# One planner, new durations, new due times: a reordered attention and feed-forward kernel

## The chip, the cores and the metric

One core of a Trainium2 chip runs the whole program. The metric is the device time of one execution in microseconds. The kernel before was timed three times: 1012.86, 1009.65 and 1012.70 us, median 1012.7 us.

## The reference

There are two computations, one behind the other.

```python
# attention with random features; q, k, v are 8 x 8 x 576 x 64, omega is 128 x 64
def phi(x):
    proj = einsum('bhsd,md->bhsm', x, omega)
    h = proj - sum(x * x, -1) / 2
    return exp(h - max(h, -1)) / sqrt(128)
q_p, k_p = phi(q * scale), phi(k * scale)
kv = einsum('bhsm,bhsd->bhmd', k_p, v);  z = sum(k_p, axis=2)
x = einsum('bhsm,bhmd->bhsd', q_p, kv) / (einsum('bhsm,bhm->bhs', q_p, z) + 1e-6)
# feed-forward on x as 4608 tokens x 512; w_in 512 x 2048, w_out 2048 x 512 (float64 inputs)
h = x @ w_in
out = where(h > 0, h, exp(min(h, 0)) - 1) @ w_out
```

## The kernel before

**What is computed where.** The attention goes by 32 pairs of heads (`pair`): load, project k and q (`project`), sum over the keys (`kv`), normalise and form the output (`finish`). The first eight pairs do it in one way (plain fp32 matmuls, L491, L665, L781), the other 24 in another (operands split in a high and a low part, L541, then L609 and L829). The feed-forward takes 3072 tokens in eight blocks of 384: for each of 16 slices of the hidden size a step does 12 matmuls of 384 columns (`layer1`, L969 to L971: high by high, high by low, low by high), ReLU, exponential and two splits on ACT and DVE, and 9 matmuls of 512 columns (`layer2`, L1003 to L1005). The first three blocks are done in two halves of eight steps each, while the weights are still converted from float64 words (`from_f64`). The last 1536 tokens go by three groups of 512 in eight steps each (`wide1`, `wide2`, L1354, L1324, L1512): a form with seven instead of eight products, of 84 matmuls of 256 columns a step. What it needs is built before it from the weights in `prepare` (tiles `rw`, `w1t`) and `prepare2` (tiles `tw`), and `fetch` brings three 512 KB weight tiles (`wp`) for each step through three buffers.

**What sets the order.** Nothing in the code above is issued where it stands. Each operation is handed to a planner, `Plan.op(engine, ns, due, fn, reads, writes, ...)`, with a duration for each engine that may do it and a due time. `Plan.order` plays a schedule through with these durations: each engine takes, whenever it is free, the ready operation with the earliest due time, if its buffers are free. Its outcome is a fixed order of instructions on each engine, and the engine for those that name another one in `alt`. The chip then runs that order. The durations come from small formulas: `mm` for matmuls, `act`, `dve`, `pool`, and single numbers at the call. The due times come from a nominal time line (`MLP0`, `SEG`, `STEP`, ...), with offsets for each stage (`PD0`, `PDS`: the pairs from the ninth on; `PREP0`, `TWO0`; `UNIT0`, `UNIT1`; `FETCH`; `AT`, `BT`: products within a step). Only their differences matter, since a due time is compared with nothing but other due times. `ALT` holds a handicap in us for each kind of operation: another engine is taken only if it ends earlier by that much. With `port=True` DVE and POOL are planned never to run such operations at the same time. DMAs are planned as 1.1 us, bytes at 360 per ns, and another 1.1 us.

Of the kernel before, what the change touches and what calls it, by code (L numbers as in the profile page):

```python
# [9 lines left out]
F32 = mybir.dt.float32  # L10
# [8 lines left out]
P = 128  # L19
# [8 lines left out]
TB = 384  # L28
NTT = TB // P
NBLK = 8  # L30
TOK0 = NBLK * TB
SB = 512
# [27 lines left out]
PREP0, PREP = -101.339, 8.8  # L60
TWO0, TWO = -37.142, 7.995
SUM = 0.873
UNIT0, UNIT1 = 0.25, 3.77
FETCH = 14.688
BT = [-0.751, -0.373, 0.719, 0.06, 0.525, 0.7, 0.865, -0.155, -0.328, 1.177, -1.344, 0.575, -1.141, 0.489]
AT = (0.0, 0.337, 0.844, 0.312, 0.229, 0.181, 0.386)

LAG = 3.4


PAIR0 = 6.45
# [221 lines left out]

ALT = dict(kv=1.96, out=2.95, conv_clamp=13.06, conv_hi=14.02, conv_sub=16.5, g_hi=12.75, g_lo=11.74, y_hi=None, y_lo=0.82, norm=18.01, p2=0.03, unit=-5.32, unit_hi=0.48, prep=0.118, part=5.545, q_hi=1.554, q_lo=14.04, neg=7.821, turn=0.31, x_hi=0.28, sq=-0.48, two=-0.272, two_hi=0.343, sum=0.079, s_hi=0.129, s_lo=0.3, zero=-0.108)

# [5 lines left out]
def mm(n, m=1):  # L301

    return m * (n / 2.4 + 2.5)

# [9 lines left out]
def pool(n):  # L314
    return 40 + 2.33 * n


@with_exitstack
def performer_elu_kernel(
# [131 lines left out]
    def project(i, nm, due):  # L451
# [14 lines left out]
        if native(i, nm):  # L466
# [11 lines left out]
            for g in range(3):  # L478
# [16 lines left out]

                op("PE", 872 if g < 2 else 240, d, mms, [*((x, a, 2) for a in range(2)), of], (p,))
                op(
# [20 lines left out]
        for a in range(2):  # L518
            r, o = slice(a * D, a * D + D), slice(D - a * D, P - a * D)
            cs = slice(a * S, a * S + S)  # L520
            parts = ((x, 0),)
            op(
                "ACT", act(S), due - 5 + a, lambda e, r=r, cs=cs: copy(e, y()[r, cs], x()[r, 0]), parts, ((y, a, "h"),),
                alt=other("y_hi", "DVE", dve(S, True)), port=True,
            )
            op(
                "POOL", pool(S), due - 4 + a,
                lambda e, r=r, o=o, cs=cs: tt(e, y()[o, cs], x()[r, 0], y()[r, cs].bitcast(F32), ALU.subtract),
                (*parts, (y, a, "h")), ((y, a, "l"),), alt=other("y_lo", "DVE", dve(S)), port=True,
            )  # L530
        for c in range(5):
# [13 lines left out]

            op("PE", mm(256, n), d, mms, [(y, a, z) for a in range(2) for z in "hl"] + ["oh", "om"], (p,))
            op(
# [13 lines left out]
            if c in (1, 4):  # L561
# [6 lines left out]

                op("POOL", 2 * pool(4), d + 1.3, bias, [sq, *((nb, g, e) for e in range(5))], ((nb, g),))
                exps(g, js, lambda j: h()[:, j, :], d + 1.5, [(h, g, e) for e in range(5)])  # L570
# [27 lines left out]
    def kv_swapped(i, due):  # L598
# [34 lines left out]

        op("POOL", 3 * pool(2 * M) + 2 * pool(M), due + 0.5, sums, parts, (zs, (zu, 1)))
        op("ACT", act(M), due + 2.8, lambda e: copy(e, zu()[:, 0], zs()[D:P, 0]), (zs,), ((zu, 0),), alt=other("kv", "DVE", dve(M, True)), port=True)
# [12 lines left out]
    def kv(i, due):  # L648
# [21 lines left out]
        parts = parts_of(i, "k")  # L670
        op("PE", 220, due, last, [*parts, v], ((p, 0), (p, 1)))
        for a in range(2):
# [16 lines left out]
    def finish(i, due):  # L689
# [25 lines left out]
        for g in range(3):  # L715
# [67 lines left out]
        d = due - 2  # L783
        op("PE", 4 * mm(S) + 200, d, mms, [*((qh, g) for g in range(3)), ("kvf", i % 2)], [p for _, _, p in halves])
        for half, (qs, n, p) in enumerate(halves):
# [28 lines left out]
    def output(i, qt, due):  # L814
# [8 lines left out]
        def mms():  # L823
# [9 lines left out]
        op(  # L833
            "PE", 4 * mm(4 * N) + 200, due, mms, [*((qt, g) for g in range(3)), *((zk, "kv", e) for e in range(4))], banks
        )
# [120 lines left out]
    def layer1(F, due):  # L956
        blk, f = STEPS[F][:2]
        o = (SLOT[blk] if blk > 2 else blk) * TB
        w = w1c.pop(F)
        p = Buf(ps, [P, 512], F32, "ph", f"ph_{F}", 2)  # L960
        e = Buf(sb, [P, TB], F32, "e", f"e_{F}", 2)
        g = gt[F] = [Buf(sb, [P, 512], F32R, "g", f"g_{F}_{z}", 6) for z in range(2)]

        def ph():
            return p()[:, 0:TB]

        def mms(c):
            wh, wl = w()[:, 0, c * P:(c + 1) * P], w()[:, 1, c * P:(c + 1) * P]
            nc.tensor.matmul(ph(), wh, xh[:, c, o:o + TB], start=(c == 0), stop=False)  # L969
            nc.tensor.matmul(ph(), wh, xl[:, c, o:o + TB], start=False, stop=False)  # L970
            nc.tensor.matmul(ph(), wl, xh[:, c, o:o + TB], start=False, stop=(c == NC - 1))  # L971

        for c in range(NC):
            reads = [("x3h", SLOT[blk], c), ("x3l", SLOT[blk], c)] if blk > 2 else [(z, k) for k in ring(blk) if k[1] == c for z in ("xh", "xl")]
            op("PE", mm(TB, 3), due + 0.5 * c, lambda c=c: mms(c), [*reads, (w, "h"), (w, "l")], (p, ("f", blk, f)) if c == 0 else (p, ("fl", blk, f)) if c == 3 else (p,))
        due += 2

        op("ACT", act(TB, True), due, lambda: nc.scalar.activation(e(), ph(), AF.Relu, scale=-1.0), (p,), (e,))  # L978
        op("ACT", act(TB), due + 0.2, lambda: nc.scalar.activation(e(), e(), AF.Exp, scale=-1.0), (e,), (e,))  # L979
# [13 lines left out]

    def layer2(F, due):
        blk, f, f0, f1 = STEPS[F]
        g = gt.pop(F)
        for tt in range(NTT):
            if f == f0:
# [188 lines left out]
    def std_x(blk, due):  # L1187

        X = [Buf(sb, [P, NJ, M], F32, "h", f"xs_{blk}_{k}", 4) for k in range(2)]

        def x(k):
            return X[k]().rearrange("p j x -> p (j x)")[:, 0:2 * TB].rearrange("p (c x) -> p c x", c=2)

        t0, o = blk * TB, SLOT[blk] * TB
        for k in range(2):
            op(
                "SP", 500, due + 0.1 * k,
                lambda k=k: nc.sync.dma_start(x(k), xd[2 * k:2 * k + 2, :, t0:t0 + TB].rearrange("c p x -> p c x")),
                [("xd", b * NHP + hp) for b in range(B) if b * S < t0 + TB and t0 < b * S + S for hp in (2 * k, 2 * k + 1)]
                + [("f", blk - 1, 11)], (X[k],), P * TB * 8,  # L1200
            )
            first = SLOT[blk] not in list(SLOT.values())[:blk - 3]
            keys = [z for z in ring(SLOT[blk]) if z[1] in (2 * k, 2 * k + 1)] if first else []
            xk = [z[:, 2 * k:2 * k + 2, o:o + TB] for z in (xh, xl)]
            heads, tails = ([(nm, SLOT[blk], c) for c in (2 * k, 2 * k + 1)] for nm in ("x3h", "x3l"))
            op(
                "ACT", act(2 * TB), due + UNIT0 + 0.5 * k, lambda e, k=k, xk=xk: copy(e, xk[0], x(k)), (X[k],),
                [*(("xh", z) for z in keys), *heads], alt=other("unit_hi", "DVE", dve(2 * TB, True)), port=True,
            )
            op(  # L1210
                "POOL", pool(2 * TB), due + UNIT0 + 0.4 + 0.5 * k,
                lambda e, k=k, xk=xk: tt(e, xk[1], x(k), xk[0].bitcast(F32), ALU.subtract), (X[k], *heads),
                [*(("xl", z) for z in keys), *tails], alt=other("unit", "DVE", dve(2 * TB)), port=True,
            )
# [487 lines left out]
```

## Time and profile before

| | |
|---|---|
| median of three executions | 1012.7 us |
| span of the profiled execution, first to last instruction | 1006.4 us |
| what lies around the span, against the median | 6.3 us |
| PE busy | 981.2 us (97%), 7806 matmuls |
| DVE, ACT, POOL busy | 842.0, 765.8, 557.6 us |
| granted TensorE clock, mean | 1.000 |

PE is the matmul engine, PEld its weight loads, DVE, ACT and POOL the vector, scalar and GpSimd engines, SP the one that issues DMAs. A matmul's duration in the trace is longer than its distance to the next one, since matmuls are pipelined and their ends are modelled: a busy PE can hide short waits. The pace of a kind of matmul is the distance from start to start in an unbroken run.

### The profile page before, as it was taken

The numbers are of one execution on the slowest core, as the hardware profiler recorded it, in microseconds if no ns is written. First come the engines' busy times: TensorE is split into PE (matmuls) and PEld (weight loads), VectorE is DVE, ScalarE is ACT, GpSimd is POOL, SyncE is SP. The second block draws the span as 40 slices with busy tenths as digits, with TensorE's granted clock in tenths as the row PEclk, the third lists the DMA queues.
The fourth block names the chain that finished last, engine by engine and source line by source line (L and its number), as shares of the span: only waits on it lengthen the run. The fifth ranks groups of instructions, "written<-read, shape, count | busy, mean of one in ns | idle before, by whom it ended". The sixth has DMA issues, their size and how long they took to land.

```text
span 1006.4 us, 24315 instructions
## 1 busy us (share of the span) xinstructions
PE 981.2 (97%) x7806; PEld 883.9 (88%) x7806; DVE 842.0 (84%) x3077; ACT 765.8 (76%) x2064; POOL 557.6 (55%) x745
## 2 busy tenths in 40 slices
PE   7999999999999999999999999999999999999997
PEld 7788788878888888888888888888789999999997
DVE  7999977887778788878888888889999889779766
ACT  7989777777668888888787778776546788777774
POOL 2667666685547767677577766684442232223221
PEclk9999999999999999999999999999999999999999
DMA  7656787757776776676666766767878876766752
GB/s 230 174 191 198 232 276 262 249 185 236 232 246 202 236 229 204 210 240 207 223 211 220 237 196 211 231 218 236 295 272 309 294 264 205 233 219 193 220 200 66
DMA packets 93264, 226.27 MB, mean 225 GB/s; under 512 B 23056, under 2 KB 35024, under 8 KB 93136
## 3 DMA queue, kind: packets, MB, share of 16 engines
q1 hardware_dynamic: 93136, 224.70, 68.8%
q8 instruction: 63, 1.03, 0.4%
q14 instruction: 65, 0.53, 0.2%
HBM read 187.43 MB, written 37.22 MB: 223 GB/s over the span
## 4 chain that ended last, share of the span: by engine, by line
PE 68%; DVE 15%; DMA 6%; ACT 5%; issue 3%; POOL 3%; SPq 1%; DVEq 0%; POOLq 0%; ACTq 0%
PE acs L1512 9%; PE ph L969 6%; PE ph L971 6%; PE acc L1003 6%; PE ph L970 6%; PE A L1354 6%; PE acc L1005 6%; PE acc L1004 6%; PE B L1354 4%; PE pkv L609 2%; PE pn L829 2%; PE ppq L541 2%; PE ppk L541 2%; DVE junk L727 1%; DVE u_w L914 1%
## 5 line engine op out<-in xcount | busy, mean ns | idle before, releaser
L969 PE MATMUL ph<-xh,w1c 128*128 128x384 f32 x512 | 176.9, 345 | 6.3 <-DVE g L990 4.4
L970 PE MATMUL ph<-xl,w1c 128*128 128x384 f32 x512 | 172.3, 336 | 1.0 <-DVE xl L794 1.0
L971 PE MATMUL ph<-xh,w1c 128*128 128x384 f32 x512 | 172.3, 336 | 0.0
L1003 PE MATMUL acc<-w2h,g 128*128 128x512 f32 x384 | 154.6, 402 | 0.1
L1005 PE MATMUL acc<-w2h,g 128*128 128x512 f32 x384 | 151.6, 395 | 0.0
L1004 PE MATMUL acc<-w2l,g 128*128 128x512 f32 x384 | 151.3, 394 | 0.0
L969 PEld LDWEIGHTS ph<-xh,w1c 128*128 128x128 f32 x512 | 96.2, 188 | 18.7 <-DVE g L990 8.5
L970 PEld LDWEIGHTS ph<-xl,w1c 128*128 128x128 f32 x512 | 96.3, 188 | 3.8 <-DVE xl L794 1.4
L978 ACT ACTIVATE e<-ph 128x384 f32<-128x384 f32 x128 | 62.5, 488 | 47.5 <-PE ph L971 47.0
L381 POOL TENSOR_TENSOR hq<-hq,den 128x512 f32<-128x512 f32 (+1 forms) x96 | 80.9, 852 | 28.7 <-DVE den L736 23.2
L971 PEld LDWEIGHTS ph<-xh,w1c 128*128 128x128 f32 x512 | 96.2, 188 | 0.0
L982 DVE SCALAR_TENSOR_TENSOR ph<-e,ph 128x384 f32<-128x384 f32 x128 | 71.3, 557 | 27.4 <-ACT e L979 26.1
L381 POOL TENSOR_TENSOR gq<-yh,gq 128x256 fp32r<-128x256 f32 x49 | 42.8, 873 | 87.0 <-ACT gq L376 76.8
L1005 PEld LDWEIGHTS acc<-w2h,g 128*128 128x128 f32 x384 | 72.0, 188 | 17.1
L1003 PEld LDWEIGHTS acc<-w2h,g 128*128 128x128 f32 x384 | 72.1, 188 | 16.2 <-issue 6.3
L727 DVE CUSTOM_DVE_ANT_0 junk<-hq,pz 128x128 f32<-128x128 f32 (+1 forms) x320 | 74.6, 279 | 12.7 <-PE pz L705 10.6
L381 POOL TENSOR_TENSOR tk<-xk,tk 64x576 fp32r<-64x576 f32 x45 | 64.1, 1424 | 32.2 <-ACT tk L376 14.9
L461 ACT ACTIVATE hk<-hk,nbk 128x128 f32<-128x128 f32 x216 | 68.4, 391 | 15.7 <-POOL nbk L567 15.3
L1004 PEld LDWEIGHTS acc<-w2l,g 128*128 128x128 f32 x384 | 72.2, 188 | 8.7
L461 ACT ACTIVATE hq<-hq,nbq 128x128 f32<-128x128 f32 x216 | 68.4, 391 | 13.5 <-POOL nbq L567 13.0
L381 POOL TENSOR_TENSOR tq<-xq,tq 64x576 fp32r<-64x576 f32 x46 | 65.9, 1432 | 21.4 <-ACT tq L376 11.1
L990 DVE TENSOR_TENSOR g<-ph,g 128x384 fp32r<-128x384 f32 x128 | 70.6, 551 | 5.7 <-PE pn L829 1.8
(222 smaller groups left out, 2816.9 us busy)
## 6 DMA issues: line engine op xcount, KB each, us to landing
w1c<-w1s SPq DMA_DIRECT2D x112, 512.0 KB, 4.4
wp<-w1t SPq DMA_DIRECT2D x48, 512.0 KB, 3.7
raw_w<-in_w_dram SPq DMA_DIRECT2D x32, 512.0 KB, 4.3
xk<-in_kx_dram SPq DMA_DIRECT2D x24, 576.0 KB, 4.6
xq<-in_qx_dram SPq DMA_DIRECT2D x24, 576.0 KB, 4.6
wp<-w1s SPq DMA_DIRECT2D x24, 512.0 KB, 4.2
v<-in_v_dram SPq DMA_DIRECT2D x32, 325.0 KB, 3.2
w1s<-w1c SPq DMA_DIRECT2D x16, 512.0 KB, 3.9
```

The source lines that it names most:

```text
L381: (nc.vector if e == "DVE" else nc.gpsimd).tensor_tensor(*args)
L461: nc.scalar.activation(h()[:, j, :], src(j), AF.Exp, bias=nb()[:, j:j + 1], scale=-1.0)
L727: nc.vector.tensor_tensor_reduce(out=junk()[r], in0=h()[r, j, :], in1=pz()[r, a * P:(a + 1) * P], scale=1.0, scalar=EPS, op0=ALU.mult, op1 ...
L969: nc.tensor.matmul(ph(), wh, xh[:, c, o:o + TB], start=(c == 0), stop=False)
L970: nc.tensor.matmul(ph(), wh, xl[:, c, o:o + TB], start=False, stop=False)
L971: nc.tensor.matmul(ph(), wl, xh[:, c, o:o + TB], start=False, stop=(c == NC - 1))
L982: lambda: nc.vector.scalar_tensor_tensor(ph(), e(), -1.0, ph(), ALU.add, ALU.max), (p, e), (p,),
L1003: nc.tensor.matmul(a(), g[0]()[:, ts], w2h[:, f], start=(f == f0), stop=False)
L1004: nc.tensor.matmul(a(), g[0]()[:, ts], w2l[:, f], start=False, stop=False)
L1005: nc.tensor.matmul(a(), g[1]()[:, ts], w2h[:, f], start=False, stop=(f == f1 - 1))
L1354: nc.tensor.matmul(o, at(a, i), u[b][:, i], start=(start and fresh_bank and i == 0 and n == 0), stop=(i == 1 and n == 2), skip_group_check ...
L1512: nc.tensor.matmul(bank()[:, z * TH:(z + 1) * TH], g()[:, a * TH + z * P:a * TH + z * P + P], w(b), start=(j == 0 and z == 0 and m == 0), ...
```

## The change

Two things are edited, and no operation, shape, buffer or dependency.

First the durations that the planner is told: all formulas for matmuls, those for POOL, and single numbers. Second all due-time constants and all handicaps, which have new values. A third edit is a renaming: the block size 384 becomes a list `BLOCKS` of eight entries of 384, and slices that were `0:TB` become `0:n` with n = 384.

```diff
-MLP0 = 37.61
-SEG = [6.25, 7.76, 3.48, 4.4, 2.75, 6.34]
-STEP = 5.52
-STEP_ATT = 5.44
-STEP_SA, STEP_S = 9.344, 8.511
-LAG2 = 1.848
-PD0, PDS = 122.22, 19.83
+MLP0 = 48.92
+SEG = [6.61, 7.799, 3.497, 4.451, 2.774, 6.427]
+STEP = 5.125
+STEP_ATT = 5.727
+STEP_SA, STEP_S = 8.818, 8.388
+LAG2 = 2.061
+PD0, PDS = 122.159, 18.9
...
-PREP0, PREP = -101.339, 8.8
-TWO0, TWO = -37.142, 7.995
-UNIT0, UNIT1 = 0.25, 3.77
-FETCH = 14.688
+PREP0, PREP = -102.36, 8.276
+TWO0, TWO = -37.736, 8.809
+UNIT0, UNIT1 = 4.467, 5.114
+FETCH = 11.628
...
-AT = (0.0, 0.337, 0.844, 0.312, 0.229, 0.181, 0.386)
+AT = (0.0, 0.433, 0.77, 0.368, 0.475, 0.153, 0.257)
...
-ALT = dict(kv=1.96, out=2.95, ... unit=-5.32, unit_hi=0.48, prep=0.118, part=5.545, ... two=-0.272, ...)
+ALT = dict(kv=0.807, out=4.797, ... unit=-6.237, unit_hi=3.546, prep=0.531, part=6.216, ... two=-0.204, ...)
...
 def mm(n, m=1):
-    return m * (n / 2.4 + 2.5)
+    return m * (0.467 * n - 6.2)
...
 def pool(n):
-    return 40 + 2.33 * n
+    return 120 + 2.22 * n
...
-op("PE", 872 if g < 2 else 240, d, mms, ...)      # project, first eight pairs
+op("PE", 930 if g < 2 else 290, d, mms, ...)
-op("POOL", pool(S), due - 4 + a, ...)              # project, the others: low part
+op("POOL", 1495, due - 4 + a, ...)
-op("PE", mm(256, n), d, mms, ...)
+op("PE", 118 * n + 10, d, mms, ...)
-op("POOL", 2 * pool(4), d + 1.3, bias, ...)
+op("POOL", 550, d + 1.3, bias, ...)
-op("PE", 5 * 216, due, mms, [*parts, v], (p,))     # kv_swapped
+op("PE", 1340, due, mms, [*parts, v], (p,))
-op("POOL", 3 * pool(2 * M) + 2 * pool(M), due + 0.5, sums, ...)
+op("POOL", 3480, due + 0.5, sums, ...)
-    "PE", 4 * mm(4 * N) + 200, due, mms, ...       # output
+    "PE", 1400, due, mms, ...
```

## Rows read from the trace of the kernel before

**Rows 1.** Windows, whole span: stretch, length, busy PE, PEld, DVE, ACT, POOL (instructions).

```profile
0.00:25.00 25.00, 19.87 (x136) 17.98 (x136) 17.48 (x52) 17.75 (x49) 6.28 (x11) 1.00 0.79 231
25.00:125.00 100.00, 96.28 (x678) 80.24 (x679) 94.36 (x319) 88.55 (x234) 67.78 (x59) 1.00 0.63 197
125.00:225.00 100.00, 96.55 (x516) 84.81 (x516) 80.98 (x228) 74.32 (x166) 69.39 (x75) 1.00 0.74 244
225.00:675.00 450.00, 449.01 (x3861) 395.00 (x3860) 365.80 (x1756) 361.28 (x1005) 308.27 (x471) 1.00 0.69 221
675.00:800.00 125.00, 119.96 (x895) 107.09 (x894) 118.62 (x311) 72.95 (x198) 49.95 (x64) 1.00 0.80 281
800.00:1001.00 201.00, 199.43 (x1727) 198.72 (x1725) 162.67 (x412) 150.92 (x417) 55.94 (x69) 1.00 0.64 204
1001.00:1006.40 5.40, 0.11 (x2) 0.00 (x0) 2.06 (x4) 0.00 (x0) 0.00 (x0) 0.97 0.44 147
```

**Rows 2.** Timeline of PE, 400 to 440 us: start, duration, instruction.

```profile
404.01 0.39 PE L1003 MATMUL acc<-w2h,g 128*128 128x512 f32 x1
...
407.27 0.40 PE L1005 MATMUL acc<-w2h,g 128*128 128x512 f32 x1
...
409.69 0.34 PE L969 MATMUL ph<-xh,w1c 128*128 128x384 f32 x1
...
412.11 0.34 PE L971 MATMUL ph<-xh,w1c 128*128 128x384 f32 x1
```

**Rows 3.** Chain that ended last: start, us, what.

```profile
407.67 1.29 PE pn L829 x64
416.95 1.24 PE pkv L609 x20
...
800.53 1.36 PE acs L1512 x12
```

**Rows 4.** Timeline of POOL, 440 to 470 us.

```profile
446.47 0.20 POOL L566 TENSOR_TENSOR nbk<-nbk,sqk 128x4 f32<-128x4 f32 x1
446.74 0.20 POOL L567 TENSOR_TENSOR nbk<-nbk,sqk 128x4 f32<-128x4 f32 x1
447.02 1.45 POOL L381 TENSOR_TENSOR tk<-xk,tk 64x576 fp32r<-64x576 f32 x1
...
464.43 1.44 POOL L381 TENSOR_TENSOR tq<-xq,tq 64x576 fp32r<-64x576 f32 x1
465.94 0.20 POOL L566 TENSOR_TENSOR nbk<-nbk,sqk 128x4 f32<-128x4 f32 x1
```

**Rows 5.** Tile pn, over the whole span: ns min/median/max, first and last start.

```profile
L829 PE MATMUL pn<-qt,zk x1536: 294/294/345, 228.0 to 717.9; 32*64 32x160 f32 x192
```

**Rows 6.** Groups by line of DVE, 675 to 800 us.

```profile
L381 DVE TENSOR_TENSOR rw<-rw 128x256 f32<-128x256 f32 (+2 forms) x41 | 24.9, 629 | 0.7 <-DMA rw<-w1s 0.7
...
L727 DVE CUSTOM_DVE_ANT_0 junk<-hq,pz 128x128 f32<-128x128 f32 (+1 forms) x20 | 4.6, 277 | 0.1
...
L807 DVE STREAM_TRANSPOSE qt<-hq 128x512 f32<-128x512 f32 (+1 forms) x8 | 3.8, 492 | 0.1
```

**Rows 7.** Tile rw: the same columns as rows 5.

```profile
L381 DVE TENSOR_TENSOR rw<-rw x43: 406/681/1227, 684.0 to 802.1; 128x256 f32<-128x256 f32 x16, 128x512 fp32r<-128x512 f32 x14, 128x512 f32<-128x512 f32 x13
...
L381 POOL TENSOR_TENSOR rw<-rw x13: 733/742/1302, 644.5 to 747.1; 128x256 f32<-128x256 f32 x8, 128x512 f32<-128x512 f32 x3, 128x512 fp32r<-128x512 f32 x2
```

**Rows 8.** Tile wp: first and last products, and its loads.

```profile
L1354 PE MATMUL A<-xh,wp x240: 276/276/357, 758.0 to 986.3; 128*128 128x256 f32 x120
...
DMA to landing us min/median/max: 3.1/3.7/6.6
```

**Rows 9.** Waits of PE: us in total, times, longest.

```profile
PE ph L969 <- DVE g L990: 4.4, 8, 1.5
...
PE A L1354 <- DMA wp<-w1t: 1.2, 1, 1.2
```

**Rows 10.** Chain at the end of the span.

```profile
1000.58 1.35 DVE c L1526 x3
1001.93 0.09 issue
1002.01 1.05 DVEq L1697
```

More of the change, by code (lines that the diff above doesn't have):

```diff
@@ L28 @@
 TB = 384
-NTT = TB // P
-NBLK = 8
-TOK0 = NBLK * TB
+BLOCKS = [TB] * 8
+NBLK = len(BLOCKS)
+START = [sum(BLOCKS[:n]) for n in range(NBLK + 1)]
+TOK0 = START[-1]
 SB = 512
@@ L290, in issue @@
             self.tasks[n][2](eng)
-ALT = dict(kv=1.96, out=2.95, conv_clamp=13.06, conv_hi=14.02, conv_sub=16.5, g_hi=12.75, g_lo=11.74, y_hi=None, y_lo=0.82, norm=18.01, p2=0.03, unit=-5.32, unit_hi=0.48, prep=0.118, part=5.545, q_hi=1.554, q_lo=14.04, neg=7.821, turn=0.31, x_hi=0.28, sq=-0.48, two=-0.272, two_hi=0.343, sum=0.079, s_hi=0.129, s_lo=0.3, zero=-0.108)
+ALT = dict(kv=0.807, out=4.797, conv_clamp=11.684, conv_hi=13.53, conv_sub=16.089, g_hi=13.458, g_lo=12.815, y_hi=None, y_lo=0.995, norm=17.509, p2=0.805, unit=-6.237, unit_hi=3.546, prep=0.531, part=6.216, q_hi=1.929, q_lo=12.076, neg=3.769, turn=1.621, x_hi=0.206, sq=-0.326, two=-0.204, two_hi=0.109, sum=0.078, s_hi=1.002, s_lo=-1.027, zero=0.265)
 def other(kind, *engs):
@@ L494, in view @@
                     return p().rearrange("p (j x) -> p j x", j=4)
-                op("PE", 872 if g < 2 else 240, d, mms, [*((x, a, 2) for a in range(2)), of], (p,))
+                op("PE", 930 if g < 2 else 290, d, mms, [*((x, a, 2) for a in range(2)), of], (p,))
                 op(
@@ L526, in project @@
             op(
-                "POOL", pool(S), due - 4 + a,
+                "POOL", 1495, due - 4 + a,
                 lambda e, r=r, o=o, cs=cs: tt(e, y()[o, cs], x()[r, 0], y()[r, cs].bitcast(F32), ALU.subtract),
@@ L544, in view @@
                 return p().rearrange("p (a x) -> p a x", a=2)
-            op("PE", mm(256, n), d, mms, [(y, a, z) for a in range(2) for z in "hl"] + ["oh", "om"], (p,))
+            op("PE", 118 * n + 10, d, mms, [(y, a, z) for a in range(2) for z in "hl"] + ["oh", "om"], (p,))
             op(
@@ L567, in bias @@
                     nc.gpsimd.tensor_tensor(m, m, q, ALU.subtract)
-                op("POOL", 2 * pool(4), d + 1.3, bias, [sq, *((nb, g, e) for e in range(5))], ((nb, g),))
+                op("POOL", 550, d + 1.3, bias, [sq, *((nb, g, e) for e in range(5))], ((nb, g),))
                 exps(g, js, lambda j: h()[:, j, :], d + 1.5, [(h, g, e) for e in range(5)])
@@ L632, in flat @@
             return zs()[0:D].rearrange("p a x -> p (a x)")
-        op("POOL", 3 * pool(2 * M) + 2 * pool(M), due + 0.5, sums, parts, (zs, (zu, 1)))
+        op("POOL", 3480, due + 0.5, sums, parts, (zs, (zu, 1)))
         op("ACT", act(M), due + 2.8, lambda e: copy(e, zu()[:, 0], zs()[D:P, 0]), (zs,), ((zu, 0),), alt=other("kv", "DVE", dve(M, True)), port=True)
@@ L670, in kv @@
         parts = parts_of(i, "k")
-        op("PE", 220, due, last, [*parts, v], ((p, 0), (p, 1)))
+        op("PE", 240, due, last, [*parts, v], ((p, 0), (p, 1)))
         for a in range(2):
@@ L783, in finish @@
         d = due - 2
-        op("PE", 4 * mm(S) + 200, d, mms, [*((qh, g) for g in range(3)), ("kvf", i % 2)], [p for _, _, p in halves])
+        op("PE", 1250, d, mms, [*((qh, g) for g in range(3)), ("kvf", i % 2)], [p for _, _, p in halves])
         for half, (qs, n, p) in enumerate(halves):
@@ L833, in output @@
         op(
-            "PE", 4 * mm(4 * N) + 200, due, mms, [*((qt, g) for g in range(3)), *((zk, "kv", e) for e in range(4))], banks
+            "PE", 1400, due, mms, [*((qt, g) for g in range(3)), *((zk, "kv", e) for e in range(4))], banks
         )
@@ L961, in layer1 @@
         e = Buf(sb, [P, TB], F32, "e", f"e_{F}", 2)
+        n = BLOCKS[blk]
         g = gt[F] = [Buf(sb, [P, 512], F32R, "g", f"g_{F}_{z}", 6) for z in range(2)]
         def ph():
-            return p()[:, 0:TB]
+            return p()[:, 0:n]
         def mms(c):
             wh, wl = w()[:, 0, c * P:(c + 1) * P], w()[:, 1, c * P:(c + 1) * P]
-            nc.tensor.matmul(ph(), wh, xh[:, c, o:o + TB], start=(c == 0), stop=False)
-            nc.tensor.matmul(ph(), wh, xl[:, c, o:o + TB], start=False, stop=False)
@@ L976, in layer1 @@
         due += 2
-        op("ACT", act(TB, True), due, lambda: nc.scalar.activation(e(), ph(), AF.Relu, scale=-1.0), (p,), (e,))
-        op("ACT", act(TB), due + 0.2, lambda: nc.scalar.activation(e(), e(), AF.Exp, scale=-1.0), (e,), (e,))
-        op(
-            "DVE", dve(TB), due + 0.8,
-            lambda: nc.vector.scalar_tensor_tensor(ph(), e(), -1.0, ph(), ALU.add, ALU.max), (p, e), (p,),
+        op("ACT", act(n, True), due, lambda: nc.scalar.activation(e()[:, 0:n], ph(), AF.Relu, scale=-1.0), (p,), (e,))
@@ L983, in layer1 @@
+        op("ACT", act(n), due + 0.2, lambda: nc.scalar.activation(e()[:, 0:n], e()[:, 0:n], AF.Exp, scale=-1.0), (e,), (e,))
+        op(
+            "DVE", dve(n), due + 0.8,
+            lambda: nc.vector.scalar_tensor_tensor(ph(), e()[:, 0:n], -1.0, ph(), ALU.add, ALU.max), (p, e), (p,),
         )
-        first, second = ("ACT", act(TB, True)), ("DVE", dve(TB))
+        first, second = ("ACT", act(n, True)), ("DVE", dve(n))
         if blk:
             first, second = second, first
-        op(*first, due + 1.2, lambda x: copy(x, g[0]()[:, 0:TB], ph()), (p,), (g[0],), alt=other("g_hi", *second))
+        op(*first, due + 1.2, lambda x: copy(x, g[0]()[:, 0:n], ph()), (p,), (g[0],), alt=other("g_hi", *second))
@@ L988, in layer1 @@
         op(
-            "DVE", dve(TB), due + 1.5,
-            lambda: nc.vector.tensor_tensor(g[1]()[:, 0:TB], ph(), g[0]()[:, 0:TB].bitcast(F32), ALU.subtract),
+            "DVE", dve(n), due + 1.5,
+            lambda: nc.vector.tensor_tensor(g[1]()[:, 0:n], ph(), g[0]()[:, 0:n].bitcast(F32), ALU.subtract),
             (p, g[0]), (g[1],),
@@ L996, in layer2 @@
         g = gt.pop(F)
-        for tt in range(NTT):
+        for tt in range(BLOCKS[blk] // P):
             if f == f0:
@@ L1197, in std_x @@
                 "SP", 500, due + 0.1 * k,
-                lambda k=k: nc.sync.dma_start(x(k), xd[2 * k:2 * k + 2, :, t0:t0 + TB].rearrange("c p x -> p c x")),
-                [("xd", b * NHP + hp) for b in range(B) if b * S < t0 + TB and t0 < b * S + S for hp in (2 * k, 2 * k + 1)]
-                + [("f", blk - 1, 11)], (X[k],), P * TB * 8,
+                lambda k=k: nc.sync.dma_start(x(k), xd[2 * k:2 * k + 2, :, t0:t0 + n].rearrange("c p x -> p c x")),
+                [("xd", b * NHP + hp) for b in range(B) if b * S < t0 + n and t0 < b * S + S for hp in (2 * k, 2 * k + 1)]
+                + [("f", blk - 1, 11)], (X[k],), P * n * 8,
             )
@@ L1203, in std_x @@
             keys = [z for z in ring(SLOT[blk]) if z[1] in (2 * k, 2 * k + 1)] if first else []
-            xk = [z[:, 2 * k:2 * k + 2, o:o + TB] for z in (xh, xl)]
+            xk = [z[:, 2 * k:2 * k + 2, o:o + n] for z in (xh, xl)]
             heads, tails = ([(nm, SLOT[blk], c) for c in (2 * k, 2 * k + 1)] for nm in ("x3h", "x3l"))
             op(
-                "ACT", act(2 * TB), due + UNIT0 + 0.5 * k, lambda e, k=k, xk=xk: copy(e, xk[0], x(k)), (X[k],),
-                [*(("xh", z) for z in keys), *heads], alt=other("unit_hi", "DVE", dve(2 * TB, True)), port=True,
+                "ACT", act(2 * n), due + UNIT0 + 0.5 * k, lambda e, k=k, xk=xk: copy(e, xk[0], x(k)), (X[k],),
+                [*(("xh", z) for z in keys), *heads], alt=other("unit_hi", "DVE", dve(2 * n, True)), port=True,
             )
             op(
-                "POOL", pool(2 * TB), due + UNIT0 + 0.4 + 0.5 * k,
+                "POOL", pool(2 * n), due + UNIT0 + 0.4 + 0.5 * k,
                 lambda e, k=k, xk=xk: tt(e, xk[1], x(k), xk[0].bitcast(F32), ALU.subtract), (X[k], *heads),
-                [*(("xl", z) for z in keys), *tails], alt=other("unit", "DVE", dve(2 * TB)), port=True,
+                [*(("xl", z) for z in keys), *tails], alt=other("unit", "DVE", dve(2 * n)), port=True,
             )
```

37 lines of the change are left out of this document (20 added, 17 removed).

## The prediction

> **What bounds the kernel now.** I read the windows first, since a mean over the span hides that the stages differ. PE is busy 981.2 of 1006.4 us, so it idles 25.2 us in all, and the windows say where [rows 1]: 25.00 - 19.87 = 5.1 us in the first 25 us, 3.7 us from 25 to 125, 3.5 us from 125 to 225, only 1.0 us in the 450 us up to 675, 5.0 us from 675 to 800, 1.6 us from there to 1001, and 5.3 us after the last matmul. The granted clock is 1.00 in every stretch with work, that is 2.4 GHz, so no order can win anything there. The reader is to see three kinds of stage. In the middle and in the last 200 us PE never waits for long. From 25 to 125 DVE is busy 94.4% and from 675 to 800 it is busy 118.6/125 = 95%: there DVE, not PE, sets the pace. The two ends are a first load and a last chain of additions [rows 10].
>
> An order can only remove waiting. The work of PE stays: 128 steps x 12 = 1536 matmuls of 384 columns at a pace of (412.11 - 409.69)/14 = 0.173 us, 1152 of 512 columns at (407.27 - 404.01)/14 = 0.233 us [rows 2], and 24 x 84 = 2016 of 256 columns at 1.36/12 = 0.113 us [rows 3]. That is 266 + 268 + 228 = 762 us; the rest is attention. So the change is worth at most the 25.2 us that show as idle and some that the modelled ends hide.
>
> **The change part by part.**
>
> *Durations of PE.* The planner of before counts n/2.4 + 2.5: 0.1625 us for 384 columns, 0.2158 for 512, 0.1092 for 256. The rows say 0.173, 0.233, 0.113. The new formula 0.467n - 6.2 gives 0.1731, 0.2329, 0.1134: it meets all three. The kv sums were planned at 1.08 us and are now at 1.34, with 1.24 in the row and a switch beside it; the output goes from 1.28 to 1.40, with 1.29 in the row and a following gap [rows 3]. Summed over the kernel the planner's PE gets longer by 512 x 32 ns = 16.3 us (layer 1), 384 x 51 ns = 19.7 us (layer 2), 2016 x 4.2 ns = 8.4 us (the last groups), 24 x (0.26 + 0.12) = 9.1 us (kv and output), and 10 us for the rest of the attention: about 64 us, 7% of some 900. The planner of before thus played a PE that was 7% too fast, and ordered its feeders for that.
>
> The Trainium skill, "TensorE: Matmul & The Clock Gate", section "Wait — 56ns, not 53.3ns?", gives just the old formula as the spacing of warm matmuls, measured there as 215.7 ns for 512 columns. By that page the old durations were right and the new ones 64 us too long, and the new plan would be the wrong one; the trace has 0.233 us in an unbroken run at full clock, so the row decides.
>
> *Durations of POOL.* The two tiny additions of a bias were planned at 2 x 49 = 99 ns; the row has 447.02 - 446.47 = 0.55 us, which is the new number. The split of 576 elements was 1382 ns, is 1495, and the row has 465.94 - 464.43 = 1.51 us [rows 4]. Over 96 biases and 96 splits that is 43 + 11 us of POOL that the old plan did not know of, besides the sums (24 x 0.9 = 21 us). None of this is on PE's path by itself: from 225 to 675 POOL is busy 68% [rows 1]. It costs nothing to run; it only tells the plan when a result is there.
>
> *The time line.* MLP0 rises by 11.3, but pairs and blocks before the first step hang on MLP0, and only differences count: no cost. What does move is the ratio of attention to feed-forward. Before, pair 32 was due 122.22 + 23 x 19.83 = 578.3 after the second segment began and the last groups 634.3 after it, 56.0 later. Now these are 122.16 + 23 x 18.9 = 556.9 and 648.1, so 91.3. The last pair is due 35 us earlier against the last groups. In the trace the last output matmul of the attention starts at 717.9 [rows 5] and the first product of the last groups at 758.0 [rows 8]: 40 us; I expect some 75. That takes DVE work out of the stretch 675 to 800, where DVE is full: L727 4.6 + L807 3.8 us are seen there [rows 6], and with the smaller groups about 12 us by my estimate. It goes into 225 to 675, where DVE has 84 us free [rows 1].
>
> *Preparing the last groups.* `prepare` keeps its due times (-101.3 to -102.4 before the groups), yet its DVE part runs from 684.0 to 802.1 [rows 7], 44 us past the first product at 758.0 [rows 8]: it is late, because DVE is full. With the attention gone earlier it can start sooner. The handicap of DVE for it rises from 0.118 to 0.531, which sends more of it to POOL, busy only 50 of 125 us [rows 1].
>
> Against this speaks that DVE and POOL hinder each other: an operation on `rw` took 406 ns at least and 1227 at most on DVE, 733 and 1302 on POOL [rows 7]. The Trainium skill, "SBUF — State Buffer", section "SBUF: two separate sides", has it that the two share one pair of ports as an exclusive lock, held for the whole instruction; by that, an addition moved from DVE to POOL would hold the pair for 0.73 instead of 0.41 us and would free nothing, and this term would be zero or a loss of 0.3 us for each one moved. The maxima fit. I therefore give the handicap nothing and count the earlier end of the attention alone.
>
> *What that brings.* Bounds by stretch: the start (5.1) is loads and the end (5.3) is a run of additions behind the last product, which DVE makes in any order: nothing, bound 1 us either way. From 25 to 225 there is 7.2 us of idle; the largest single wait of PE is for the low half of the activations, 4.4 us in 8 times [rows 9]. A plan with true paces sees such waits and fills them, but conversion, attention and first steps still all need DVE: I take 3.0, between 0 and 7.2. From 675 to 800: between 0 and 5.0; I take 3.0, for the 12 us of DVE that leave. From 225 to 675 nothing. From 800 on: between 0 and 1.6, I take 0.5, part of the one wait for a `wp` load [rows 9].
>
> *Fetching.* `FETCH` falls from 14.69 to 11.63, and product 6 moves from 0.386 to 0.257 of a step, 1.1 us earlier, while product 4 moves from 0.229 to 0.475, so its tile is kept longer. Fewer margins, on SP's queue behind x loads and outputs. Where buffers decide anyway, it costs nothing; bound 24 steps x 1.2 us = 29 us. I take 0, because only one of 72 loads held PE up [rows 9]. `UNIT0` and `UNIT1` issue the loads of x 9.6 instead of 4.0 before a block: SP work that is otherwise idle, bound +-1 us. The handicaps that are left pick between DVE, ACT and POOL where PE does not wait: nothing. `BLOCKS` changes no instruction: nothing.
>
> **Sum.** 3.0 + 3.0 + 0.5 = 6.5 us. The profiled span goes from 1006.4 to 999.9; with the 6.3 us around it, 1006.2 us against the median of 1012.7.
>
> **The rivals.**
>
> *No change that shows.* The middle 650 us idle 2.6 us in all [rows 1], and the waits that are left are set by DVE's work, which the order does not shrink. For it: DVE at 94 to 95% in both bad stretches. Against it: 84 us free on DVE right between them. Time: 1012.7.
>
> *Lost margin, the other side.* A plan with a PE 7% too fast asks for everything 7% earlier than the real PE needs it, and this margin covered what the planner misjudges. The place is the `wp` load in the last groups. The planner counts 1.1 + 1.46 + 1.1 = 3.66 us for it; the rows have 3.1 to 6.6 with a median of 3.7 [rows 8], so half the loads are later than planned. PE takes its instructions in order, so a late tile holds up every product and output behind it, and ACT and DVE behind those. It decides when a load lands after the product that now stands 1.1 us earlier. If a quarter of the 24 steps pay the one wait seen, 1.2 us [rows 9], that is 7 us, and with no gain elsewhere 1012.7 + 7 = 1020. For it: the spread. Against it: over 200 us with 1.6 us of idle.
>
> *Attention crowds the middle.* If 225 to 675 came to look like 25 to 125 with DVE over 90%, it would idle 3.7 us in each 100: 16.7 - 1.0 = 15.7 us, less the 6.5 gained, so 1022. Against it: 7% more pairs there bring DVE from 81% to some 86%.
>
> *The old durations right.* Then the new plan errs by as much the other way; the old one's idle between 25 and 1001 is 14.8 us, and as much again gives 1027. The paces in rows 2 and 3 speak against it. The page on the matmul, named above, would have it so.
>
> **How the numbers follow.** The forecast 0.56, no change 0.24, lost margin 0.12, a crowded middle 0.06, old durations right 0.02. A measurement here can tell about 0.3%, 3 us, from nothing: the forecast's own range, 998 to 1009.5, lies below that bound, its low end being all 14.8 us of idle won back. So faster 0.56, same 0.24, slower 0.20. The range reaches from 998 to 1019, just short of the lost margin's 1020, which leaves out its upper half and the two cases behind it.
>
> **What would show it.** Right: last output matmul of the attention 60 us or more before the first product of the last groups; `prepare` on DVE over before 790; idle PE from 675 to 800 at 3 us or less and from 25 to 225 at 5 or less; paces as before. Wrong: waits of L1354 for `wp` above 3 us in all (lost margin), idle above 3 us from 225 to 675 (crowding), or the same idle in the same stretches (no change).

## The result, and the profile after

The changed kernel takes 1022.27 us (median of four executions, 1020.99 to 1025.14) beside 1011.17 (1009.38 to 1012.86) for the kernel before: a ratio of 1.0124 with a 95% interval of [1.0097, 1.0152], a small loss that is clear of noise, where 1006.2 us and a gain were forecast. Its profiled span is 1018.9 us, 12.5 longer, at a granted clock of 0.999.

The engines' busy time on the page of the kernel after (us, share of the span, instructions):

```profile
PE 987.8 (97%) x7806; PEld 885.2 (87%) x7806; DVE 836.5 (82%) x2997; ACT 781.7 (77%) x2147; POOL 557.9 (55%) x742
```

Its windows, same columns as [rows 1] and behind them clock, DMA share and GB/s:

```profile
0.00:25.00 25.00, 20.80 (x143) 18.84 (x144) 16.37 (x48) 18.06 (x51) 6.65 (x11) 1.00 0.82 242
25.00:125.00 100.00, 94.59 (x663) 78.21 (x664) 87.88 (x296) 90.73 (x240) 69.68 (x59) 1.00 0.62 199
125.00:225.00 100.00, 93.72 (x498) 81.41 (x497) 81.98 (x219) 72.11 (x160) 56.84 (x61) 1.00 0.70 234
225.00:675.00 450.00, 445.72 (x3900) 389.29 (x3899) 359.59 (x1757) 376.10 (x1093) 314.95 (x484) 1.00 0.67 216
675.00:800.00 125.00, 121.86 (x795) 108.07 (x795) 111.33 (x247) 64.10 (x158) 50.84 (x56) 1.00 0.79 277
800.00:1013.00 213.00, 210.44 (x1811) 208.94 (x1810) 176.77 (x430) 160.62 (x449) 58.98 (x72) 1.00 0.65 208
```

The reader is to see that the same 7806 matmuls ran at the same clock, and that PE now idles 5.4 us from 25 to 125 (3.7 before), 6.3 from 125 to 225 (3.5) and 4.3 from 225 to 675 (1.0). Besides the first 25 us (4.2 instead of 5.1) only 675 to 800 got better: 3.1 instead of 5.0. All idle is 31.1 us, 5.9 more than before; that is half of the 12.5. The rest hides under the modelled ends of matmuls. Take as the pace of a matmul the median distance to the next start over all matmuls of its tiles and shape in both traces. What goes beyond it sums up to 73.7 us before and 86.3 after, which accounts for the whole 12.5: 9.4 of it between 125 and 450 us, 3.7 from 450 to 675, 2.5 after 800, and -3.5 from 675 to 800.

Waits of PE in the kernel after, as in [rows 9]; its lines stand one to three further down:

```profile
PE ph L971 <- DVE g L992: 5.6, 10, 0.9
...
PE ppk L542 <- DVE nbk L556: 1.6, 1, 1.6
PE ppk L542 <- DVE nbq L556: 1.5, 1, 1.5
PE pt L752 <- ACT hq L462: 1.5, 1, 1.5
...
PE A L1357 <- DMA wp<-w1t: 0.5, 1, 0.5
```

One step of its chain, as in [rows 3]:

```profile
862.65 1.36 PE acs L1515 x12
```

Its tile `pn`, as in [rows 5]:

```profile
L830 PE MATMUL pn<-qt,zk x1536: 294/294/346, 232.9 to 697.6; 32*64 32x160 f32 x192
```

Its tile `wp`, as in [rows 8]:

```profile
L1357 PE MATMUL A<-xh,wp x240: 276/276/393, 767.3 to 999.5; 128*128 128x256 f32 x120
...
DMA to landing us min/median/max: 3.1/4.1/6.5
```

Its tile `rw`, as in [rows 7]:

```profile
L382 POOL TENSOR_TENSOR rw<-rw x30: 728/914/1299, 673.6 to 817.5; 128x256 f32<-128x256 f32 x24, 128x512 f32<-128x512 f32 x4, 128x512 fp32r<-128x512 f32 x2
L382 DVE TENSOR_TENSOR rw<-rw x26: 673/692/1517, 682.0 to 824.9; 128x512 fp32r<-128x512 f32 x14, 128x512 f32<-128x512 f32 x12
```

The attention ends 767.3 - 697.6 = 70 us before the last groups (40 before), paces are as before (1.36 us for 12 matmuls), and the wait for `wp` fell from 1.2 to 0.5 us. The waits that grew are many, short and spread: PE on DVE and ACT together 13.3 -> 20.2 us between 25 and 1000, none over 1.6 us.

### The profile page after: what moved, and what is told of

Same layout as the page of the kernel before. It is cut to its first block, busy times and chain, and to the rows that moved or that the text cites. A ratio compares the mean times of both kernels' runs of the same rounds, so it can differ in the third digit from the quotient of the medians.

```text
span 1018.9 us, 24328 instructions
## 1 busy us (share of the span) xinstructions
PE 987.8 (97%) x7806; PEld 885.2 (87%) x7806; DVE 836.5 (82%) x2997; ACT 781.7 (77%) x2147; POOL 557.9 (55%) x742
## 3 DMA queue, kind: packets, MB, share of 16 engines
q8 instruction: 63, 1.03, 0.4%
## 4 chain that ended last, share of the span: by engine, by line
PE 57%; DVE 15%; DMA 10%; ACT 10%; issue 4%; POOL 3%; SPq 1%; DVEq 0%; POOLq 0%; ACTq 0%
PE acs L1515 7%; PE ph L971 6%; PE ph L973 5%; PE ph L972 5%; PE acc L1005 5%; PE A L1357 5%; PE acc L1006 5%; PE acc L1007 5%; PE B L1357 4%; PE pn L830 2%; PE ppq L542 2%; PE pkv L610 2%; PE ppk L542 2%; DMA xk<-in_kx_dram 2%; DMA raw_w<-in_w_dram 2%
## 5 line engine op out<-in xcount | busy, mean ns | idle before, releaser
L382 POOL TENSOR_TENSOR gq<-yh,gq 128x256 fp32r<-128x256 f32 x48 | 39.8, 830 | 141.5 <-ACT gq L377 117.4
L1005 PEld LDWEIGHTS acc<-w2h,g 128*128 128x128 f32 x384 | 72.1, 188 | 15.7 <-issue 5.4
L462 ACT ACTIVATE hq<-hq,nbq 128x128 f32<-128x128 f32 x216 | 68.5, 393 | 10.7 <-POOL nbq L568 10.1
L918 POOL TENSOR_TENSOR u_w<-u_w,raw_w 128x512 int32<-128x512 int32 x32 | 45.1, 1412 | 54.4 <-DVE u_w L915 34.8
L382 POOL TENSOR_TENSOR tq<-xq,tq 64x576 fp32r<-64x576 f32 x43 | 61.6, 1432 | 21.9 <-ACT tq L377 9.3
```

The source lines that it names most:

```text
L382: (nc.vector if e == "DVE" else nc.gpsimd).tensor_tensor(*args)
L462: nc.scalar.activation(h()[:, j, :], src(j), AF.Exp, bias=nb()[:, j:j + 1], scale=-1.0)
L1005: nc.tensor.matmul(a(), g[0]()[:, ts], w2h[:, f], start=(f == f0), stop=False)
```

## Experiments

Ratios are to the kernel before, run on the same chip, with a 95% interval. The theories, as the expectations name them: **lost margin** (a PE planned too fast is needed), **new due times** (attention earlier is to blame), **misfit** (due times fit only the durations that they were searched with), **uneven correction** (PE and POOL made true, ACT and DVE left too fast), **luck of the draw**.

### One half of the change at a time

`e1` is before with the new durations, `e11` before with those of PE alone, `e2` after with the old durations (the reverse of the diff's second half).

> The kernel before with the new planner durations alone (matmuls, POOL, the single numbers); due times and handicaps as before. Theory 1, lost margin: true durations order everything just in time, so most of the loss comes with them, 1018 to 1025 us. Theory 2, the new due times are to blame (attention drawn forward, products moved within a step): durations alone do no harm, 1006 to 1014. Theory 3, each set of due times only fits the durations it was searched with, and any other order near it costs: 1015 to 1025 here, and the same with the other mix.

> The kernel after with the old planner durations; due times and handicaps new. Theory 1, lost margin: a PE planned 7% too fast restores the margin, 1008 to 1014. Theory 2, the due times: as slow as the kernel after, 1018 to 1026. Theory 3, a misfit of due times and durations: 1018 to 1030, slower than before as the other mix is.

> Before with the new durations of PE alone; those of POOL, ACT and DVE and all due times as before. Theory 4: the most uneven of all mixes, the three feeders are planned too fast against PE: 1040 to 1065, slower than e1 (1039), in which POOL is true. Theory 3: as the other mixes, 1030 to 1042. Theory 1: 1030 to 1040, as e1.

Measured: e1 1038.88 us, 1.0313 [1.0270, 1.0356]; e2 1037.70, 1.0292 [1.0265, 1.0318]; e11 1044.96, 1.0344 [1.0309, 1.0380]. Either half alone costs 3%, more than both together, and e1 and e2 lie above every range that was given for them. So halves can't be added up: new durations with old due times tell nothing about the durations, and neither half can be called the cause from these runs.

### The attention's place alone

`e3` is before with the attention due earlier, `e4` after with it due later again.

```diff
-PD0, PDS = 122.22, 19.83     # e3, before
+PD0, PDS = 122.22, 18.295
-PD0, PDS = 122.159, 18.9     # e4, after
+PD0, PDS = 122.159, 20.434
```

> The kernel before with one number changed: PDS 19.83 to 18.295, so that the last pair is due 91.3 instead of 56.0 us before the last groups, as in the kernel after. Theory 2 in its form 'attention crowds the middle': slower by 5 to 10, 1016 to 1021, with idle PE from 225 to 675 of 4 us or more. Theory 1: margin untouched, within 4 us of before. Theory 3: any shift costs, 1014 to 1022.

> The kernel after with one number changed: PDS 18.9 to 20.434, so that the last pair is due 56.0 us before the last groups, as in the kernel before. Crowded middle: most of the loss comes back, 1012 to 1016. Lost margin: as after, 1019 to 1025. Theory 3: a misfit to its own search, 1022 to 1032.

Measured: e3 1007.65 us, 0.9984 [0.9968, 1.0000]; e4 1026.38, 1.0179 [1.0150, 1.0209]. Windows of e3, two stretches:

```profile
225.00:675.00 450.00, 447.27 (x3972) 390.88 (x3971) 375.29 (x1810) 359.94 (x1031) 321.83 (x489) 1.00 0.68 219
675.00:800.00 125.00, 121.36 (x769) 109.86 (x768) 112.63 (x257) 69.38 (x176) 28.75 (x34) 1.00 0.83 294
```

DVE takes 9.5 us more in the middle and 6.0 less behind it than in [rows 1]; PE's idle falls by 1.4 us there and rises by 1.7 in the middle. The move is harmless, and taking it back heals nothing: new due times in this sense are refuted. Since e3 stays below the 1014 us of a misfit, not every shift of due times costs. The products' places within a step (`AT`) and `FETCH` were not moved alone.

### One nanosecond

`j3` is before, `k3` after, with one nanosecond on every DVE duration, which is far less than the spread of what such an operation takes (0.41 to 0.97 us in the DVE row below).

```diff
-    return 69 + n / ...
+    return 70 + n / ...
```

> Before with 1 ns more in the duration formula of DVE (70 instead of 69 ns), nothing else. No margin and no engine's pace changes by this. Theory 3 in its sharp form, the searched due times give a good order only with exactly the durations they were searched with: 1025 to 1040. Theories 1 and 4 in pure form: 1007 to 1014, as before.

> The kernel after with 1 ns more in the formula of DVE, the counterpart of j3_one_nanosecond. Theory 3 (a searched set of due times fits only its own durations to the nanosecond): 1028 to 1040. Otherwise as after, 1018 to 1026.

Measured: j3 1036.48 us, 1.0257 [1.0217, 1.0298]; k3 1027.54, 1.0166 [1.0134, 1.0198]. Tile `gq` of before (low parts in the last groups; ns least/median/most, first and last start, shapes), on POOL and on DVE:

```profile
L381 POOL TENSOR_TENSOR gq<-yh,gq x49: 723/799/1704, 768.7 to 992.6; 128x256 fp32r<-128x256 f32 x49
...
L381 DVE TENSOR_TENSOR gq<-yh,gq x47: 410/420/967, 774.1 to 997.4; 128x256 fp32r<-128x256 f32 x47
```

The same rows of j3:

```profile
L381 POOL TENSOR_TENSOR gq<-yh,gq x83: 729/764/1186, 790.7 to 1029.3; 128x256 fp32r<-128x256 f32 x83
...
L381 DVE TENSOR_TENSOR gq<-yh,gq x13: 417/425/427, 813.1 to 1020.9; 128x256 fp32r<-128x256 f32 x13
```

Here one sees a cliff. Half of these 96 splits have a handicap of 0.300 us (`s_lo`), and for them it is close: DVE is planned at 335.67 ns, with the handicap 635.67, against 636.48 on POOL. One nanosecond more tips the tie, and 34 of these splits go to POOL (83 instead of 49), 0.76 instead of 0.42 us each. That this shift makes all of the 2.6% isn't shown; other orders moved too. What is shown: with before's due times and handicaps one nanosecond in the durations costs as much as any effect looked for. With after's it does little that shows: k3 lies 0.4% above the kernel after, with overlapping intervals and between its two ranges. What decides below are sets searched for their own durations.

### What the new durations leave wrong

For each planned operation of a trace I took the distance to the next start on its engine, where the next one's inputs had been there for 0.45 us or more, and divided the sum by the planned sum. In brackets stands the median of the same quotient over the single operations:

| | PE | ACT | DVE | POOL |
|---|---|---|---|---|
| before | 1.11 (1.08) | 1.17 (1.03) | 1.15 (1.00) | 1.23 (1.10) |
| after | 1.05 (1.00) | 1.15 (1.02) | 1.17 (1.00) | 1.07 (1.01) |
| s2 (below) | 1.06 (1.00) | 1.13 (1.01) | 1.15 (1.00) | 1.06 (1.01) |
| o22 (below) | 1.11 (1.08) | 1.11 (1.01) | 1.18 (1.00) | 1.22 (1.10) |
| s1 (below) | 1.04 (1.00) | 1.04 (0.94) | 1.06 (0.92) | 1.03 (1.00) |

The sums shift by up to 0.08 with how strictly waits for a free buffer or another engine are left out; at the strictest, before has 1.10, 1.09, 1.10, 1.22 and after 1.03, 1.09, 1.11, 1.05. By the sums, the old durations are too short on all engines, POOL's most. The new ones repair PE and POOL, and leave ACT and DVE, so that PE, 0.04 to 0.06 below these two before, is 0.10 to 0.12 below them after. The medians tell it otherwise. The old durations of ACT and DVE already fit the typical operation; PE and POOL alone were planned 8 and 10% too short, and in the kernel after the typical operation is planned right on all four engines. What makes ACT and DVE long in the sum is a part of their operations: about one in six on DVE and one in three on ACT takes over 10% more than planned. Timeline of ACT in the kernel after (start, duration, instruction):

```profile
702.20 0.49 ACT L980 ACTIVATE e<-ph 128x384 f32<-128x384 f32 x1
702.72 0.53 ACT L981 ACTIVATE e<-e 128x384 f32<-128x384 f32 x1
703.15 0.39 ACT L377 CAST w_t<-tw 128x256 fp32r<-128x256 f32 x1
```

Timeline of DVE in the same kernel:

```profile
880.45 0.42 DVE L1381 TENSOR_TENSOR c<-B,c 128x256 f32<-128x256 f32 x1
881.00 0.27 DVE L1312 MEMSET B<- 128x256 f32 x1
...
883.79 0.41 DVE L382 TENSOR_TENSOR y<-yh,y 128x256 f32<-128x256 f32 x1
884.12 0.41 DVE L382 TENSOR_TENSOR gq<-yh,gq 128x256 fp32r<-128x256 f32 x1
884.46 0.41 DVE L382 TENSOR_TENSOR yh<-yh 128x256 f32<-128x256 f32 x1
```

The ReLU of `ph` takes 702.72 - 702.20 = 0.52 us to the next start, planned 0.37; the addition of `B` 0.55, planned 0.34. But the next operation needs what these two made: the exponential reads the ReLU's `e`, and the `MEMSET` clears the `B` that the addition read. For such a pair the planner adds 0.20 us on ACT and 0.13 on DVE (`LAT`), so it plans 0.57 and 0.46. These two rows don't show durations that are too short. The splits of 256 columns behind them keep 0.33 to 0.34 us, as planned. The long ones are of another sort: in the row of `rw` on DVE above, operations of 512 columns are planned at 0.60 us. A row's duration is some 0.08 us longer than the distance to the next start (0.41 against 0.33 here), so the median of 0.69 fits the plan, and the longest, 1.52, is far off it.

`e5` (before's due times) and `e6` (after's) have the new durations and, in `Plan.op`, 45 ns more for each ACT and 38 for each DVE operation:

```diff
-        engs = {eng: (ns, 0.0)}
-        for e, *t in alt or ():
-            engs[e] = tuple(t)
+        more = dict(ACT=45, DVE=38)
+        engs = {eng: (ns + more.get(eng, 0), 0.0)}
+        for e, t, late in alt or ():
+            engs[e] = t + more.get(e, 0), late
```

> Due times and handicaps of before, the new durations for PE and POOL, and besides them 45 ns more for each planned operation on ACT and 38 ns more for each on DVE, so that all four engines are planned about as slow as they run. Only these two numbers differ from e1_new_durations (1039 us). Theory 4, uneven correction (PE and POOL were made true, ACT and DVE are still planned too fast, so feeders are planned too late): most of e1's loss comes back, 1005 to 1018. Theory 3, due times only fit the durations they were searched with: 1025 to 1045, as both mixes so far. Theory 1, a PE planned too fast is a margin that is needed: 1025 to 1040, since PE stays as planned in e1.

> The kernel after with the same 45 ns (ACT) and 38 ns (DVE) more for each planned operation; its due times and handicaps were searched without them. Theory 4, uneven correction: faster than after, 1003 to 1015. Theory 3, misfit: slower than after, 1025 to 1040. Theory 1: as after, 1018 to 1026.

Measured: e5 1025.94 us, 1.0157 [1.0130, 1.0185]; e6 1022.64, 1.0134 [1.0104, 1.0163]. With before's due times the correction of ACT and DVE takes back half of e1's loss; with after's it changes nothing. Uneven correction had forecast at most 1018 and 1015 us and missed both; both times lie in the ranges of lost margin. Neither is decisive, as neither set was searched for these durations.

### Searched anew, for three sets of durations

The due times and handicaps are drawn at random, 11,000 to 16,000 times a search, and kept by where the planner's own schedule ends (`s3`: by its order played through with traced durations). The sets: *PE and POOL true* (after's durations: s2, u11, u12), *all four longer* (e6's: s1, s3, c11, c12), *all four too short* (before's own: o21, o22). s1, s2, c11, u11 start from before's due times, the others from after's.

```diff
-STEP_SA, STEP_S = 9.344, 8.511        # s1: nearly all constants get new values, such as
-LAG2 = 1.848
-PD0, PDS = 122.22, 19.83
+STEP_SA, STEP_S = 10.279, 11.131
+LAG2 = 5.238
+PD0, PDS = 123.376, 18.563
```

> The planner durations of e6 (PE and POOL as in the kernel after, ACT +45 ns and DVE +38 ns for each operation), and due times and handicaps searched anew for them: 16,000 random changes from the values of before, kept by the plan's own end. Theory 4, uneven correction: what the kernel after lost is its slow ACT and DVE, and a search that is told of them does not spend their time twice: 985 to 1010, faster than after by 12 or more, perhaps faster than before. Theory 5, luck of the draw (any searched order lands some 10 us around its place, and before was a good draw): 1010 to 1028, like after. Theory 1, a PE planned too fast is needed: 1015 to 1028.

> The planner durations of the kernel after, unchanged (ACT and DVE too fast), and due times and handicaps searched anew by the same search, from the same start and with as many draws as s1. It is a second draw of what the change did. Theory 4: 1015 to 1027, like after and slower than s1 by 12 or more. Theory 5: anywhere from 1003 to 1028, without order against s1.

> Durations of e6 again, due times and handicaps searched from the values of after, with an order kept by how it ends when ACT and DVE operations take what the traces of the earlier runs show for each kind. Theory 4: as s1 or a little better, 982 to 1008. Theory 5: 1005 to 1025.

> A second search with the durations of e6 (ACT and DVE as slow as they run), other draws, from the due times of before. Theory 4, uneven correction: near s1's 1004, 1000 to 1014. Theory 5, luck of the draw: anywhere from 1003 to 1030.

> A third search with the durations of e6, from the due times of the kernel after. Theory 4: 1000 to 1014, so 10 or more faster than after with a start from after's own values. Theory 5: 1003 to 1030; a start that decides: 1018 to 1028, near after.

> A second search with the durations of the kernel after, from the due times of before, as many draws as c11. Theory 4: 1018 to 1032, slower than c11. Theory 5: anywhere from 1003 to 1030.

> A third search with the durations of the kernel after, from its own due times. Theory 4: 1016 to 1030, slower than c12. Theory 5: anywhere from 1003 to 1030.

> Before's durations, which are too short on all four engines by 11 to 23% of the distances in its trace; due times and handicaps searched anew in some 11,000 draws, from the changed kernel's. Uneven correction: what a search needs is errors that are alike on all engines, not durations that are true, so this ends with the three searches on all four engines' corrected durations: 1000 to 1015 us. Durations must be true: 1015 to 1035 us, at or above the searches with PE and POOL alone corrected. Before is a lucky draw: this one lands anywhere from 1005 to 1030.

> The same as the run before it with another seed. Uneven correction: 1000 to 1015 us. Durations must be true: 1015 to 1035 us. Lucky draw: anywhere from 1005 to 1030, and the two may differ by 15 us.

| durations | kernel | us | ratio |
|---|---|---|---|
| PE and POOL true | after | 1022.27 | 1.0124 [1.0097, 1.0152] |
| | s2 | 1029.28 | 1.0203 [1.0174, 1.0232] |
| | u11 | 1028.41 | 1.0209 [1.0170, 1.0247] |
| | u12 | 1018.74 | 1.0115 [1.0070, 1.0159] |
| all four longer | s1 | 1004.50 | 0.9947 [0.9927, 0.9967] |
| | s3 | 1017.67 | 1.0078 [1.0056, 1.0099] |
| | c11 | 1017.02 | 1.0084 [1.0057, 1.0111] |
| | c12 | 1016.74 | 1.0095 [1.0061, 1.0130] |
| all four too short | o21 | 1014.13 | 1.0058 [1.0035, 1.0081] |
| | o22 | 1012.36 | 1.0043 [1.0020, 1.0066] |

All four with PE and POOL true lie above all six others: 1.0163 on average, against 1.0051 (all four longer) and 1.0051 (all four too short). So what separates the groups is not whether PE's durations are true: they are in s1 and not in o22. That three searches of nine land in the last three places happens by chance once in 84. From before's start the gap is 1.2 to 2.6% (s2, u11 over s1, c11), from after's 0.2 to 0.7% (u12 over s3, c12, o21, o22), and c12 and u12 overlap: it shows in the groups, not in each pair. Uneven correction also missed ranges here: s3, c11 and c12 came out at 1017 us, above the 1008, 1014 and 1014 that it allowed, and s2 2 us above its own. No search here has POOL's durations changed by themselves, so their part isn't told apart.

Two readings of the gap remain. *Uneven correction*: by the sums, ACT and DVE are planned too fast against PE in the slow group. *Lost margin*, taken widely: by the medians, the slow group is the one that plans the typical operation right, while both others plan ACT and DVE some 5 to 8% slow against PE, the old durations by a short PE (1.08 against 1.00 to 1.03), the 45 and 38 ns by long ACT and DVE (1.00 against 0.92 to 0.94). Both readings name the same relation of PE to ACT and DVE, and no set here separates them.

How two draws with the same start and search differ, windows from 225 to 675; s1:

```profile
225.00:675.00 450.00, 449.25 (x3991) 394.07 (x3990) 366.16 (x1790) 372.99 (x1088) 320.19 (x494) 1.00 0.69 224
```

and s2:

```profile
225.00:675.00 450.00, 441.54 (x3842) 377.44 (x3841) 400.65 (x1911) 348.44 (x947) 270.61 (x446) 1.00 0.66 212
```

s2 lets DVE, which it takes for cheap, work 400.7 of 450 us where s1 gives it 366.2, and takes 50 us from POOL; PE idles 8.5 us there against 0.8. But that isn't the mark of an uneven plan. The kernel after doesn't show it (DVE 359.6), nor does u11 (357.6), and c11, which has s1's durations and start, does, with 5.5 us of idle PE:

```profile
225.00:675.00 450.00, 444.46 (x3955) 388.11 (x3954) 390.97 (x1817) 368.63 (x1066) 266.86 (x445) 1.00 0.67 215
```

One way that is left, and not shown, is that ACT and DVE deliver later than a now slower PE is planned for. The waits of PE on the two between 25 and 1000 us are 20.2, 13.5, 22.0 and 10.7 us in the four uneven kernels and 7.8 to 15.7 in the seven even ones with before: it points that way and doesn't settle it.

s1 beats both kernels: 0.53% under before, 1.7% under after. Its windows from 25 to 225, where before has 7.2 us of idle and after 11.7, have 6.1:

```profile
25.00:125.00 100.00, 95.51 (x685) 79.95 (x684) 89.61 (x320) 90.03 (x243) 68.26 (x62) 1.00 0.58 190
125.00:225.00 100.00, 98.40 (x532) 87.75 (x531) 81.48 (x228) 75.78 (x164) 71.88 (x73) 1.00 0.73 250
```

It is one draw of four, so it is a find, not the worth of those durations.

## Why the prediction was wrong

**The paces of PE and POOL** were read rightly: over the operations of the trace after, the median error of the new numbers is 0.00 us on PE and 0.01 on POOL. The *old durations right* rival is out by these paces (1.36 us for 12 matmuls before and after), though searches with the old durations do as well as those with all four longer.

**The step that failed** is "A plan with true paces sees such waits and fills them", the 3.0 us for 25 to 225, and with it "From 225 to 675 nothing". Idle from 25 to 225 rose by 4.5 us (7.2 to 11.7) and in the middle by 3.3. The 4.4 us that PE waits for `g` in [rows 9] are of the whole span; 3.3 of them lie in that stretch, and after the change 2.8. So that wait hardly moved, and others came beside it, for `nbk` (1.6), `nbq` (1.5) and `hq` (1.5), short ones on DVE and ACT. The premise was not looked at: I held PE and POOL against rows and asked nothing of ACT and DVE, which make nearly all that PE waits for. A plan that is true for PE and for the typical operation of the others still isn't true: in the sum ACT and DVE take 1.15 and 1.17 of their planned time, and nothing in the new plan covers for it. Before, PE was planned at 1/1.11 in the sum, close to these two. That this relation of PE to its feeders is what the change spoiled fits the three groups of searches. It isn't shown by a cause that can be followed in a trace, and which of the two readings above is right stays open.

**A second step, left out**, was to ask what another draw of the same search is worth. o21 and o22 have before's durations and are 0.4 and 0.6% slower than before. By that, some 0.5 of the 1.24% is that before is a better draw than a fresh one, and the other 0.7 is the durations; with a spread this wide the split is an estimate. How the constants of either kernel were found, no run shows.

**Earlier attention** went as forecast: 70 us instead of some 75 of lead, and idle from 675 to 800 at 3.1 us. The last operation of `prepare` on DVE began at 824.9, not before 790. All 24 additions of 256 columns went to POOL, at a median of 0.80 us, against 0.74 for the eight that were there before. The 406 to 1227 ns that the prediction read in [rows 7] mix two shapes: on DVE 256 columns took 406 to 967, 512 columns 678 to 1227. From 800 on 1.0 us was lost where 0.5 was to be won, at the start 0.9 won.

**The rivals.** *Lost margin* had the sign and 1020 us, but not the place: `wp` held PE up for 0.5 us. Read widely, as a loss of slack against ACT and DVE, it is not refuted: the searches with all four longer are no test against it, since 45 and 38 ns more give ACT and DVE a margin by themselves. It is the rival that is left. *Attention crowds the middle* had 1022 and the idle there (4.3 us), but DVE had less work there than before (359.6 against 365.8 us), and e3 shows the move harmless. *No change* is out by the interval. The range ended at 1019, since I gave cases with a loss 0.20; one nanosecond can cost 2.6% (j3), so a wholly new set of constants deserved far more.

## What to carry to other kernels

A planner that only compares engines lives by the proportion of their durations. Correcting two of four shifts it, and with it the margin between them, even if each single correction is right; so measure all engines at once before correcting some. Say by which measure a duration is true: DVE was right by the median and 17% short by the sum in one and the same trace. Constants searched against a planner can hang on its numbers to the last nanosecond, so halves of such a change can't be judged alone; search anew for each, several times, and compare groups. Before forecasting a gain from a reordering, ask how far two draws of the same search lie apart; here that is 1.5% (s1 and c12), as much as all 14.8 us of idle that could be won back.

## What the runs showed that was not expected

Mean and median part company on the feeders. In the kernel after the middle half of the DVE operations that had their inputs early lies within 7 ns of the plan, and yet their sum is 11 to 17% above it, by how strictly waits are left out; ACT's is 9 to 15%. And splits moved from DVE to POOL by a tie of 0.81 ns come with some 26 us on the whole, though POOL is busy only 115 of the last 230 us in j3:

```profile
800.00:1030.00 230.00, 225.78 (x1927) 222.81 (x1926) 178.30 (x396) 169.55 (x473) 114.91 (x146) 1.00 0.64 209
```
